# Column sums of phi(k) read from two Strassen operand sums instead of from phi(k)

## The chip, the cores and the metric

The kernel runs on one core of a Trainium2 chip. The metric is device time in microseconds (us); the time of a kernel is the median of its runs, and one further execution is taken by the hardware profiler. The engines are named as the profile names them: PE (matmuls), PEld (the loading of a matmul's weights), DVE (vector engine), ACT (scalar engine), POOL, and SP, whose queue issues nearly all transfers.

## What is computed

Two linear attention blocks, A and B, work on the same x and are mixed by a gate:

```python
g = sigmoid((x * gate_w).sum(-1))                 # x: 2048 x 640, bf16
# for each block, with its own wqkv (640 x 1920) and wo (640 x 640), 32 heads of 20 columns:
q, k, v = split(x @ wqkv)
phi = lambda t: where(t > 0, t + 1, exp(t)) + 1e-6
pq, pk = phi(q), phi(k)
kv  = pk^T v          # per head, 20 x 20
z   = column sums of pk over the 2048 rows, per head
o   = (pq kv) / (pq z + 1e-6)
out = g * (o_A @ wo_A) + (1 - g) * (o_B @ wo_B)
```

## The kernel before

**Stages.** The rows are cut into 16 tiles of 128 (`ST`), the 640 columns into 5 of 128 (`DT`) or two halves of 320 (`HF`). For A, then for B, PE runs through the same stages, in an order written out by hand (`manual_schedule`, lines 704 to 806), and each engine takes its own instructions strictly in that order.

1. `k_chunk` (line 218): k = x wk, ten 128x320 matmuls a tile; `phi` (197) turns it into `pk`, with an exponential on ACT and two operations on DVE.
2. `q_pass` (644): `q_unit` (253) makes 128 columns of q for 1024 rows in ten 128x512 matmuls, and `phi` writes them to `pqT`. A unit called with `lifted` takes its "+1" on ACT (line 202) and has a cheaper second DVE operation (205); otherwise DVE reads PSUM itself (207). A has five units left here, B has ten.
3. The column sums. `z_rows` (370), called in `q_pass` behind the first unit, multiplies a 128x32 tile of ones with each of the 16 row tiles of `pk` and each column half: 32 matmuls, four side by side in four groups of 32 columns of the PE array. DVE then multiplies the sums with the head mask `E4` (line 381) into `zr`. `z_pass` (387), two units later, spreads `zr` with five small matmuls, and DVE copies that to `zsel` (395), the weights of `rec_pass` (468), which makes the denominators ("den"). In A, `gate_pass` (179) stands between the first unit and `z_rows`; it makes the gate's sums ("lg") and their exponentials `ge`.
4. `g_all` (669): G = x^T pk (640 x 640). `g_pass` (281) does the fifth block of columns of x plainly, 32 matmuls. `g_strassen` (323) does the other four by Strassen's scheme in Winograd's form, as seven products of 16 matmuls (`g_prod`, 314), in the order x11 b11, SX2 TK2, x12 b21, SX3 TK3, SX1 TK1, x22 TK4, SX4 b22. The operand sums of x are `SX[1..4]` (`x_sum`, 296, made once, in A) and those of pk are `TK[1..4]` (`k_sum`, 306, made in each block), all by DVE; a `k_sum` has 2560 elements to a partition, an `x_sum` 2048. Between the second and the third product stand eight matmuls of `norm_spread` ("ex", 518).
5. `kv_a` and `m_a` for A (among the k tiles of B), `kvt_mm` (398) and `m_unit` (450) for B: products with wv and wo. `kvt_mm(1, ...)` is the first work of PE behind B's `g_strassen`; its weights are `wvB`.
6. The output, in pairs of row tiles (class `Pair`, 558).

**PSUM** has four slots that `ps` (67) hands out in turn or by number; a slot is free when whoever reads it has done so.

**Buffers of the weights.** `wpool` has one buffer to each tag. A's weights and B's share a tag, so a transfer to B's weights waits until the last reader of the tag's former tile is done. Before, `wvB` is issued on SP behind `kv_a` (line 721) and `woB` at line 725, ahead of B's `q_pass`. `TK` of A lies in `pqT[1]`, still empty then; `TK` of B lies in `xT` (2, 3, 4), and its `TK1` in the buffer of wk.

Of the kernel before, what the change touches and what calls it, by code (L numbers as in the profile page):

```python
# [8 lines left out]
P = 128  # L9
FP32 = mybir.dt.float32  # L10
BF16 = mybir.dt.bfloat16
ACT = mybir.ActivationFunctionType
ALU = mybir.AluOpType
# [9 lines left out]
TW = 4  # L23
# [10 lines left out]
def kernel(  # L34
# [32 lines left out]
    def ps(name, slot=None):  # L67

        return ps_raw(name, slot).bitcast(FP32).rearrange("p (b n) -> p b n", b=2)
# [8 lines left out]
    wo_sb = [None, None]  # L78
    ident = persist.tile([P, P], BF16, name="ident")
    I4 = persist.tile([P, H], BF16, name="I4")  # L80
    E4 = persist.tile([P, D], BF16, name="E4")
    maskE = persist.tile([P, WB[0]], BF16, name="maskE")
    KVA = persist.tile([P, NW, WB[0]], BF16, name="KVA")
    spread = persist.tile([P, P], BF16, name="spread")
# [6 lines left out]
    def flat(t, pattern, inner, at=0):  # L91
        n = hc * inner
        return t[:].rearrange(pattern)[:, at * n:(at + 1) * n].rearrange("p (i n) -> p i n", i=hc)
# [1 line left out]
    S3 = persist.tile([P, 3, hc, ic], BF16, name="S3")  # L95
    SX = {k: S3[:, k - 1] for k in (1, 2, 3)}
    SX[4] = flat(M[1], "p c d -> p (c d)", ic)
    TK = [{k: flat(pqT[1], "p c s -> p (c s)", HF, k - 1) for k in (1, 2, 3, 4)},
          {k: flat(xT, "p c s -> p (c s)", HF, k - 2) for k in (2, 3, 4)}]
    ma_dram = scratch.tile([D, D], BF16, name="ma_dram")  # L100
    lift = persist.tile([P, 1], FP32, name="lift")
    TM = [persist.tile([P, DT, HF], BF16, name="TM0")] + [None] * 3
# [46 lines left out]
    for sign, base in ((1, 0), (-1, Dh - 1)):  # L149
# [1 line left out]
            out=maskE[:], in_=maskE[:], pattern=[[-sign * Dh, WB[0] // Dh], [0, Dh]],  # L151
            compare_op=ALU.is_ge, fill=0.0, base=base, channel_multiplier=sign,
        )
    nc.gpsimd.memset(E4[:], 1.0)
    for r in range(4):
        rows = slice(32 * r, 32 * r + 32)
        for sign, base in ((1, 0), (-1, Dh - 1)):
            nc.gpsimd.affine_select(
                out=E4[rows], in_=E4[rows], pattern=[[sign, D]],
                compare_op=ALU.is_ge, fill=0.0, base=base, channel_multiplier=-sign * Dh,  # L160
            )


    warm = ps("warm", 3)
# [13 lines left out]

    def gate_pass():

        pt = ps("lg")
        for h in range(2):
            by_group(pt[:, 0, h * RB:(h + 1) * RB], gwr, xT, h)
        for b in range(2):
            nc.scalar.activation(out=ge[b][:], in_=pt[:, 0, :], func=ACT.Exp, scale=(-1.0, 1.0)[b])
            nc.vector.tensor_scalar(ge[b][:], ge[b][:], 1.0, 1e30, op0=ALU.add, op1=ALU.min)

    def x_transpose(i, slot, eng, cuts=(0, DT)):
# [60 lines left out]
    def mixed(t, m):  # L249

        return t[:, m::DT]
# [29 lines left out]
    def g_pass(b, c, slot):  # L281

        pt = ps(f"g{'AB'[b]}", slot)
        for i in range(ST):
            for hf in range(2):
                g_mm(c, i, hf, pt)
        for hf in range(2):
            nc.scalar.copy(out=GT[hf][:, c, :], in_=pt[:, hf, 0:HF])

    def g_mm(c, i, hf, pt):  # L290
        nc.tensor.matmul(  # L291
# [4 lines left out]
    def x_sum(k):  # L296

        x11, x21 = [xn[:, 0:hc, n:n + ic] for n in (0, ic)]
        x12, x22 = [xn[:, hc:ST, n:n + ic] for n in (0, ic)]
        a, b, op = {  # L300
            1: (x21, x22, ALU.add), 2: (SX[1], x11, ALU.subtract),
            3: (x11, x21, ALU.subtract), 4: (x12, SX[2], ALU.subtract),
        }[k]
        add_rows(SX[k], a, b, op)

    def k_sum(b, k):

        b11, b12 = [pk[:, 0:hc, n * HF:(n + 1) * HF] for n in range(2)]
        b21, b22 = [pk[:, hc:ST, n * HF:(n + 1) * HF] for n in range(2)]
        t = TK[b]  # L310
        left, right = {1: lambda: (b12, b11), 2: lambda: (b22, t[1]), 3: lambda: (b22, b12), 4: lambda: (b21, t[2])}[k]()
        add_rows(t[k], left, right, ALU.subtract)

    def g_prod(pt, left, right, first):

# [7 lines left out]
    def g_strassen(b, norm):  # L323

        x11, x12 = [xn[:, k:k + hc, 0:ic] for k in (0, hc)]
        x22 = xn[:, hc:ST, ic:2 * ic]
        b11 = pk[:, 0:hc, 0:HF]
        b21, b22 = [pk[:, hc:ST, n * HF:(n + 1) * HF] for n in range(2)]
        lo, hi = GT

        def temp(name):
            return work.tile([P, 2, HF], FP32, tag="osb", name=name, bufs=3)

        def add(dst, pt, sb):
            nc.vector.tensor_tensor(out=dst, in0=pt[:, :, 0:HF], in1=sb[:], op=ALU.add)

        even, odd = ps("gs0", 0), ps("gs1", 1)
        g_prod(even, x11, b11, True)
        p1 = temp("p1")
        nc.scalar.copy(out=p1[:], in_=even[:, :, 0:HF])  # L340
        g_prod(odd, SX[2], TK[b][2], True)
        u2 = temp("u2")
        add(u2[:], odd, p1)
        k_sum(b, 4)
        norm()
        g_prod(even, x12, b21, False)
        nc.scalar.copy(out=lo[:, 0:2, :], in_=even[:, :, 0:HF])
        scale(b, 0)
        scale(b, 1)
        g_prod(odd, SX[3], TK[b][3], False)  # L350
        u3 = temp("u3")
        add(u3[:], odd, p1)
        if b == 0:
            x_sum(4)
        else:
            scale(b, 2)
        even = ps("gs0", 0)
        g_prod(even, SX[1], TK[b][1], True)
        add(hi[:, 2:4, :], even, u3)
        scale(b, 3 if b else 2)  # L360
        g_prod(odd, x22, TK[b][4], False)
        add(lo[:, 2:4, :], odd, p1)
        scale(b, 4 if b else 3)
        g_prod(even, SX[4], b22, False)
        for n in range(2):
            nc.vector.tensor_tensor(out=hi[:, n, :], in0=even[:, n, 0:HF], in1=u2[:, n], op=ALU.add)
        if b == 0:
            scale(b, 4)

    def z_rows(b):  # L370

        pt = ps(f"z{'AB'[b]}")
        for k in range(ST // 4):
            for hf in range(2):
                for j in range(4):
                    nc.tensor.matmul(
                        pt[32 * j:32 * j + 32, hf, 0:HF], lhsT=ones[:], rhs=pk[:, 4 * k + j, hf * HF:(hf + 1) * HF],
                        start=(k == 0), stop=(k == ST // 4 - 1), tile_position=(0, 32 * j),
                    )
        zr = work.tile([P, D], BF16, tag="zr", name="zr")  # L380
        nc.vector.tensor_tensor(
            out=zr[:].rearrange("p (b n) -> p b n", b=2), in0=pt[:, :, 0:HF],
            in1=E4[:].rearrange("p (b n) -> p b n", b=2), op=ALU.mult,
        )
        return zr

    def z_pass(b, zr):

        pt = ps(f"zs{'AB'[b]}")
        for c in range(DT):  # L390
            nc.tensor.matmul(
                pt[:, 0, c * H:(c + 1) * H], lhsT=mixed(zr[:], c), rhs=I4[:], start=True, stop=True,
            )
        zsel = work.tile([P, DT, H], BF16, tag="zsel", name="zsel")
        nc.vector.tensor_copy(out=zsel[:], in_=pt[:, 0, 0:DT * H].rearrange("p (c h) -> p c h", h=H))
        return zsel

    def kvt_mm(b, pt, hf):
# [87 lines left out]
    def add_rows(dst, a, b, op):  # L486
        nc.vector.tensor_tensor(out=dst, in0=a, in1=b, op=op)  # L487
# [153 lines left out]
        wo_sb[b] = wpool.tile([P, NG, D], BF16, tag="wo", name="woB")  # L641
        eng.dma_start(out=wo_sb[b][:KG], in_=wo_dram[b].rearrange("(j p) f -> p j f", p=KG))

    def q_pass(b, units):

        units = list(units)
        q_unit(b, *units.pop(0))
        if b == 0:
            gate_pass()
        zr = z_rows(b)  # L650
        for k in range(2):
            if b == 0:
                x_sum(1 + k)
            q_unit(b, *units.pop(0), b == 0)
        zsel = z_pass(b, zr)
        for k, (m, h) in enumerate(units):
            if b == 0 and k < 2:
                if k:
                    x_sum(3)
                else:  # L660
                    k_sum(0, 2)
            q_unit(b, m, h, b == 0)
            if b == 1 and k == 0:
                k_sum(1, 1)
        if b == 1:
            k_sum(1, 2)
        return zsel

    def g_all(b, zsel):

        g_pass(b, DT - 1, 1)
        k_sum(b, 3)
        rts = rec_pass(b, zsel, 2)
        g_strassen(b, lambda: norm_spread(b, rts, (2, 3)))

# [27 lines left out]

    with tc.manual_schedule():
        k_chunk(0, ST - 2)
        turn[0] = (turn[0] + 1) % 4
        nc.vector.tensor_copy(out=gwr[:], in_=gcol[:, :, None].to_broadcast([P, DT, H]))
        k_chunk(0, ST - 1)
        k_sum(0, 1)
        zsel = q_pass(0, [(m, 1) for m in range(DT)])  # L710
        wq[1] = load_w(1, "q", nc.sync)
        g_all(0, zsel)

        turn[0] = 1
        for i in range(ST):
            k_chunk(1, i)
            if i > 3 and i % 2 == 0:
                m_a(i // 2 - 2)
            if i == 1:
                kv_a()  # L720
                wv[1] = load_w(1, "v", nc.sync)
            if i in (3, 6, 9, 12):
                r0 = (i - 3) // 3 * RB
                p_diff(slice(r0, r0 + RB))
        load_wo(1, nc.sync)
        t1 = wpool.tile([P, hc, HF], BF16, tag="wk", name="T1")
        TK[1][1] = t1[:]
        zsel = q_pass(1, [(m, h) for h in range(2) for m in range(DT)])
        g_all(1, zsel)
        banks.close()  # L730
        outer = ctx.enter_context(late_pool("outer"))
        TM[3] = wpool.tile([P, DT, HF], BF16, tag="wk", name="TM3")
# [104 lines left out]
```

## Time and profile before

| what | value |
|---|---|
| runs | 190.49, 190.9 and 191.43 us, median 190.9 us |
| profiled execution | 191.42 us, its span 189.7 us |
| PE busy | 184.0 us, 97% of the span |
| DVE busy | 152.7 us, 80% |
| ACT busy | 70.5 us, 37% |
| POOL busy | 8.6 us, all in the first two of 40 slices |
| granted PE clock, mean | 0.998 |
| DMA | 15.63 MB; at most 5 GB/s in each slice from 109 to 156 us |

How to read it: the span runs from the first to the last instruction of the profiled execution, 1.7 us less than its time. All times of instructions are counted from the span's start. "Busy" counts an engine from the start of an instruction to its end. Neighbouring instructions of DVE overlap by some 0.08 us, so what one costs in a full queue is the distance from its start to the next one's start, which is a little less than its duration.

### The profile page before, as it was taken

To read this page: it belongs to the slowest core of one execution; us is meant where nothing else is said; L and a number is where in the kernel's file an instruction comes from. 1 tells how busy PE (TensorE), PEld (TensorE's weight loads), DVE (VectorE), ACT (ScalarE), POOL (GpSimd) and SP (SyncE) were. 2 spreads that over 40 slices of the span, in tenths; PEclk is the share of its full clock that TensorE was granted. 3 is DMA by queue.
4 is the path that set the end of the run, shared out by engine and by line. 5 is a ranking of instruction groups with operands and counts; after the bars stand their busy time and mean duration, and the time that the engine had idled before them with its cause. 6 is when DMAs were issued, how large, how long until landed. Compare 5 with 4: busy or idle time off the path is not lost.

```text
span 189.7 us, 3630 instructions
## 1 busy us (share of the span) xinstructions
PE 184.0 (97%) x1490; PEld 124.7 (66%) x1497; DVE 152.7 (80%) x244; ACT 70.5 (37%) x99; POOL 8.6 (5%) x23
## 2 busy tenths in 40 slices
PE   8799999999999999999999999999999999999992
PEld 3566657765567677877775555576777776777771
DVE  1378968899898999789886689799999989787553
ACT  2055446455953500357672445412401611111110
POOL 8900000000000000000000000000000000000000
PEclk9999999999999999999999999999999999999999
DMA  5976438993050000241116600000000003212112
GB/s 181 324 143 87 88 78 273 343 224 101 2 173 0 3 0 0 42 166 32 54 40 218 146 5 0 0 0 3 0 0 3 3 0 108 99 65 77 69 69 73
DMA packets 19802, 15.63 MB, mean 82 GB/s; under 512 B 9546, under 2 KB 19658, under 8 KB 19786
## 3 DMA queue, kind: packets, MB, share of 16 engines
q1 hardware_dynamic: 18922, 14.59, 28.5%
q10 hardware_dynamic: 864, 0.82, 1.3%
q8 instruction: 11, 0.18, 0.4%
q14 instruction: 5, 0.04, 0.1%
HBM read 10.00 MB, written 3.44 MB: 71 GB/s over the span
## 4 chain that ended last, share of the span: by engine, by line
PE 93%; DMA 3%; DVE 1%; ACTq 0%; issue 0%; ACT 0%; DVEq 0%
PE gs L318 16%; PE kB L210 11%; PE qB L259 11%; PE kA L210 11%; PE qA L259 7%; PE ox L548 6%; PE oy L548 5%; PE oz L548 5%; PE qA L270 4%; DMA xn<-in_A_x_dram 3%; PE ow L548 3%; PE gB L291 2%; PE gA L291 2%; DVE osb L553 1%; PE mA L441 1%; PE mid L402 1%
## 5 line engine op out<-in xcount | busy, mean ns | idle before, releaser
L210 PEld LDWEIGHTS <-xT 128*128 128x128 bf16 x320 | 31.0, 98 | 12.3 <-DVE xT L195 0.4
L203 DVE TENSOR_SCALAR e<-e 128x640 bf16<-128x640 bf16 (+1 forms) x52 | 18.8, 361 | 9.6 <-ACT e L200 9.0
L210 PE MATMUL kB<-wkB,xT 128*128 128x320 bf16 x160 | 23.0, 299 | 0.0
L210 PE MATMUL kA<-wkA,xT 128*128 128x320 bf16 x160 | 22.6, 299 | 0.0
L259 PE MATMUL qB<-xT,wqB 128*128 128x512 bf16 x97 | 22.0, 379 | 0.2
L200 ACT ACTIVATE e<-kB 128x640 bf16<-128x640 f32 x16 | 11.3, 704 | 18.8 <-PE kB L210 17.5
L259 PEld LDWEIGHTS <-wqB 128*128 128x128 bf16 x100 | 11.6, 118 | 9.6 <-issue 0.3
L200 ACT ACTIVATE e<-kA 128x640 bf16<-128x640 f32 x16 | 11.1, 704 | 13.6 <-PE kA L210 13.6
L200 ACT ACTIVATE e<-qB 128x1024 bf16<-128x1024 f32 x10 | 10.2, 1024 | 13.2 <-PE qB L259 10.7
L207 DVE SCALAR_TENSOR_TENSOR pk<-kA,e 128x640 bf16<-128x640 f32 x16 | 13.2, 824 | 1.7
L207 DVE SCALAR_TENSOR_TENSOR pk<-kB,e 128x640 bf16<-128x640 f32 x16 | 13.2, 824 | 1.7
L200 ACT ACTIVATE e<-qA 128x1024 bf16<-128x1024 f32 x10 | 10.2, 1024 | 10.6 <-PE qA L259 5.2
L259 PE MATMUL qA<-xT,wqA 128*128 128x512 bf16 x58 | 13.5, 380 | 0.1
L207 DVE SCALAR_TENSOR_TENSOR pqTB<-qB,e 128x1024 bf16<-128x1024 f32 x10 | 12.2, 1224 | 1.0
L318 PEld LDWEIGHTS <-S 128*128 128x128 bf16 x96 | 9.4, 98 | 3.6
L318 PEld LDWEIGHTS <-xn 128*128 128x128 bf16 x96 | 9.1, 98 | 4.0 <-issue 0.4
L592 ACT COPY u<-ox 128x320 f32<-128x320 f32 x8 | 3.4, 426 | 21.9 <-PE ox L548 21.9
L259 PEld LDWEIGHTS <-wqA 128*128 128x128 bf16 x60 | 6.9, 118 | 5.6 <-issue 0.3
L548 PEld LDWEIGHTS <-xT 128*128 128x128 bf16 x85 | 8.0, 98 | 3.1 <-DVE xT L487 0.2
L548 PEld LDWEIGHTS <-pqTA 128*128 128x128 bf16 x85 | 7.9, 98 | 2.9 <-issue 0.2
L548 PEld LDWEIGHTS <-pqTB 128*128 128x128 bf16 x80 | 7.8, 98 | 3.0
L576 ACT COPY p1s<-ox 128x320 f32<-128x320 f32 x8 | 3.4, 426 | 16.6 <-PE ox L548 16.6
(121 smaller groups left out, 287.7 us busy)
## 6 DMA issues: line engine op xcount, KB each, us to landing
out_dram<-osb SPq DMA_DIRECT2D x14, 160.0 KB, 1.8
xn<-in_A_x_dram SPq DMA_DIRECT2D x3, 640.0 KB, 7.2
wqA<-in_A_wqkv_dram SPq DMA_DIRECT2D x1, 800.0 KB, 6.5
wvA<-in_A_wqkv_dram SPq DMA_DIRECT2D x1, 800.0 KB, 11.0
wkB<-in_B_wqkv_dram SPq DMA_DIRECT2D x1, 800.0 KB, 5.8
wqB<-in_B_wqkv_dram SPq DMA_DIRECT2D x1, 800.0 KB, 4.5
wvB<-in_B_wqkv_dram SPq DMA_DIRECT2D x1, 800.0 KB, 4.6
MA<-ma_dram SPq DMA_DIRECT2D x1, 800.0 KB, 4.4
```

The lines of the kernel that those rows point to most:

```text
L200: nc.scalar.activation(out=e[:], in_=src, func=ACT.Exp)
L203: nc.vector.tensor_scalar(e[:], e[:], 1.0, EPS, op0=ALU.min, op1=ALU.add)
L207: nc.vector.scalar_tensor_tensor(out=dst, in0=src, scalar=1.0 + EPS, in1=e[:], op0=ALU.add, op1=ALU.max)
L210: nc.tensor.matmul(pt[:, hf, 0:HF], lhsT=xT[:, c, i * P:(i + 1) * P], rhs=wk[b][:, c, hf * HF:(hf + 1) * HF], start=(c == 0), stop=(c == D ...
L259: nc.tensor.matmul(pt[:, u, :], lhsT=mixed(wq[b][:, c, :], m), rhs=xT[:, c, n * HB:(n + 1) * HB], start=(c == 0), stop=(c == DT - 1),)
L270: nc.tensor.matmul(pt[:, u, :], lhsT=mixed(wq[b][:, c, :], m + u), rhs=xT[:, c, n * HB:(n + 1) * HB], start=(c == 0), stop=(c == DT - 1),)
L291: nc.tensor.matmul(pt[:, hf, 0:HF], lhsT=xn[:, i, c * P:(c + 1) * P], rhs=pk[:, i, hf * HF:(hf + 1) * HF], start=(i == 0), stop=(i == ST - 1),
L318: nc.tensor.matmul(pt[:, n, 0:HF], lhsT=left[:, i, n * P:(n + 1) * P], rhs=right[:, i, :], start=(first and i == 0), stop=(i == hc - 1), s ...
L402: nc.tensor.matmul(pt[:KG, hf, j * KG:(j + 1) * KG], lhsT=wv[b][:, c, (4 * hf + j) * KG:(4 * hf + j + 1) * KG], rhs=GT[hf][:, c, j * KG:(j ...
L548: nc.tensor.matmul(dst, lhsT=left[:, c, r0:r0 + P], rhs=right[:, c, :], start=(first and c == 0), stop=(c == DT - 1), skip_group_check=not ...
L576: nc.scalar.copy(out=self.p1s[:], in_=self.at("x"))
L592: nc.scalar.copy(out=self.u2[:], in_=self.at("x"))
```

## The change

The column sums are no longer taken from `pk`. Two operand sums of Strassen's scheme hold them already, once the signs are turned: with b11, b12, b21, b22 the quarters of pk (first digit: half of the rows; second: half of the columns), TK3 is now b22 + b12 and TK4 is now b11 + b21 - b12 - b22. The column sums of TK3 are those of the right half of pk, and those of TK3 + TK4 are those of the left half. Both have eight row tiles, not 16, so `z_rows` has 16 matmuls. For the products to stay what they were, SX1, SX2 and SX3 change their signs too.

- `z_rows` and `z_pass` move from `q_pass` into `g_pass`: the first behind 12 of its 32 matmuls, the second behind 28. In A, `x_sum(1)`, `gate_pass` and `x_sum(2)` follow `z_rows` there, and `x_sum(3)` moves behind the second product of `g_strassen`.
- The sums come out of PSUM by two ACT copies of 128x320 and one DVE addition of 128x320. The head mask is applied behind `z_pass`, by a DVE multiplication with `headE` (128x32) in the place of the copy to `zsel`; `E4` and its eight selections on POOL go.
- All four `k_sum`s of a block are now made inside `q_pass`, before `g_pass`. In B, three of ten units are lifted.
- B's TK1 lies in the buffer of wv, TK2 and TK3 in that of wo, TK4 in that of wk. So `woB` is now issued behind the fourth product of B's `g_strassen` (SX3 TK3) and `wvB` behind the fifth (SX1 TK1).

The diff, without the parts that only rename or delete a tile:

```diff
@@ -95,8 +95,7 @@
-    TK = [{k: flat(pqT[1], "p c s -> p (c s)", HF, k - 1) for k in (1, 2, 3, 4)},
-          {k: flat(xT, "p c s -> p (c s)", HF, k - 2) for k in (2, 3, 4)}]
+    TK = [{k: flat(pqT[1], "p c s -> p (c s)", HF, k - 1) for k in (1, 2, 3, 4)}, {}]
@@ -151,14 +150,12 @@
             out=maskE[:], in_=maskE[:], pattern=[[-sign * Dh, WB[0] // Dh], [0, Dh]],
             compare_op=ALU.is_ge, fill=0.0, base=base, channel_multiplier=sign,
         )
-    nc.gpsimd.memset(E4[:], 1.0)
-    for r in range(4):
-        rows = slice(32 * r, 32 * r + 32)
-        for sign, base in ((1, 0), (-1, Dh - 1)):
-            nc.gpsimd.affine_select(
-                out=E4[rows], in_=E4[rows], pattern=[[sign, D]],
-                compare_op=ALU.is_ge, fill=0.0, base=base, channel_multiplier=-sign * Dh,
-            )
+    nc.gpsimd.memset(headE[:], 1.0)
+    for sign, base in ((1, 0), (-1, TW - 1)):
+        nc.gpsimd.affine_select(
+            out=headE[:], in_=headE[:], pattern=[[-sign * TW, H]],
+            compare_op=ALU.is_ge, fill=0.0, base=base, channel_multiplier=sign,
+        )
 
 
     warm = ps("warm", 3)
@@ -178,11 +175,11 @@
 
     def gate_pass():
 
-        pt = ps("lg")
+        pt = ps("lg", 2)
         for h in range(2):
-            by_group(pt[:, 0, h * RB:(h + 1) * RB], gwr, xT, h)
+            by_group(pt[:, 1, h * RB:(h + 1) * RB], gwr, xT, h)
         for b in range(2):
-            nc.scalar.activation(out=ge[b][:], in_=pt[:, 0, :], func=ACT.Exp, scale=(-1.0, 1.0)[b])
+            nc.scalar.activation(out=ge[b][:], in_=pt[:, 1, :], func=ACT.Exp, scale=(-1.0, 1.0)[b])
             nc.vector.tensor_scalar(ge[b][:], ge[b][:], 1.0, 1e30, op0=ALU.add, op1=ALU.min)
 
     def x_transpose(i, slot, eng, cuts=(0, DT)):
@@ -282,10 +279,19 @@
 
         pt = ps(f"g{'AB'[b]}", slot)
         for i in range(ST):
+            if i == 6:
+                zt, zr = z_rows(b, 0)
+                if b == 0:
+                    x_sum(1)
+                    gate_pass()
+                    x_sum(2)
+            if i == 14:
+                zsel = z_pass(zt, zr)
             for hf in range(2):
                 g_mm(c, i, hf, pt)
         for hf in range(2):
             nc.scalar.copy(out=GT[hf][:, c, :], in_=pt[:, hf, 0:HF])
+        return zsel
 
     def g_mm(c, i, hf, pt):
         nc.tensor.matmul(
@@ -298,8 +304,8 @@
         x11, x21 = [xn[:, 0:hc, n:n + ic] for n in (0, ic)]
         x12, x22 = [xn[:, hc:ST, n:n + ic] for n in (0, ic)]
         a, b, op = {
-            1: (x21, x22, ALU.add), 2: (SX[1], x11, ALU.subtract),
-            3: (x11, x21, ALU.subtract), 4: (x12, SX[2], ALU.subtract),
+            1: (x21, x22, ALU.subtract), 2: (x11, SX[1], ALU.subtract),
+            3: (x21, x11, ALU.subtract), 4: (x12, SX[2], ALU.subtract),
         }[k]
         add_rows(SX[k], a, b, op)
 
@@ -309,7 +315,7 @@
         b21, b22 = [pk[:, hc:ST, n * HF:(n + 1) * HF] for n in range(2)]
         t = TK[b]
         left, right = {1: lambda: (b12, b11), 2: lambda: (b22, t[1]), 3: lambda: (b22, b12), 4: lambda: (b21, t[2])}[k]()
-        add_rows(t[k], left, right, ALU.subtract)
+        add_rows(t[k], left, right, ALU.add if k in (2, 3) else ALU.subtract)
 
     def g_prod(pt, left, right, first):
 
@@ -341,13 +347,16 @@
         g_prod(odd, SX[2], TK[b][2], True)
         u2 = temp("u2")
         add(u2[:], odd, p1)
-        k_sum(b, 4)
+        if b == 0:
+            x_sum(3)
         norm()
         g_prod(even, x12, b21, False)
         nc.scalar.copy(out=lo[:, 0:2, :], in_=even[:, :, 0:HF])
         scale(b, 0)
         scale(b, 1)
         g_prod(odd, SX[3], TK[b][3], False)
+        if b == 1:
+            load_wo(1, nc.sync)
         u3 = temp("u3")
         add(u3[:], odd, p1)
         if b == 0:
@@ -356,6 +365,8 @@
             scale(b, 2)
         even = ps("gs0", 0)
         g_prod(even, SX[1], TK[b][1], True)
+        if b == 1:
+            wv[1] = load_w(1, "v", nc.sync)
         add(hi[:, 2:4, :], even, u3)
         scale(b, 3 if b else 2)
         g_prod(odd, x22, TK[b][4], False)
@@ -367,32 +378,35 @@
         if b == 0:
             scale(b, 4)
 
-    def z_rows(b):
-
-        pt = ps(f"z{'AB'[b]}")
-        for k in range(ST // 4):
-            for hf in range(2):
+    def z_rows(b, slot):
+
+        pt = ps(f"z{'AB'[b]}", slot)
+        for k in range(hc // 4):
+            for hf, t in enumerate((TK[b][4], TK[b][3])):
                 for j in range(4):
                     nc.tensor.matmul(
-                        pt[32 * j:32 * j + 32, hf, 0:HF], lhsT=ones[:], rhs=pk[:, 4 * k + j, hf * HF:(hf + 1) * HF],
-                        start=(k == 0), stop=(k == ST // 4 - 1), tile_position=(0, 32 * j),
+                        pt[32 * j:32 * j + 32, hf, 0:HF], lhsT=ones[:], rhs=t[:, 4 * k + j, :],
+                        start=(k == 0), stop=(k == hc // 4 - 1), tile_position=(0, 32 * j),
                     )
         zr = work.tile([P, D], BF16, tag="zr", name="zr")
-        nc.vector.tensor_tensor(
-            out=zr[:].rearrange("p (b n) -> p b n", b=2), in0=pt[:, :, 0:HF],
-            in1=E4[:].rearrange("p (b n) -> p b n", b=2), op=ALU.mult,
-        )
-        return zr
-
-    def z_pass(b, zr):
-
-        pt = ps(f"zs{'AB'[b]}")
+        upper = work.tile([P, HF], FP32, tag="ex", name="zu")
+        nc.scalar.copy(out=upper[:], in_=pt[:, 1, 0:HF])
+        nc.scalar.copy(out=zr[:, HF:D], in_=pt[:, 1, 0:HF])
+        nc.vector.tensor_tensor(out=zr[:, 0:HF], in0=pt[:, 0, 0:HF], in1=upper[:], op=ALU.add)
+        return pt, zr
+
+    def z_pass(pt, zr):
+
+        dst = pt[:, 0, HF:HF + DT * H]
         for c in range(DT):
             nc.tensor.matmul(
-                pt[:, 0, c * H:(c + 1) * H], lhsT=mixed(zr[:], c), rhs=I4[:], start=True, stop=True,
+                dst[:, c * H:(c + 1) * H], lhsT=mixed(zr[:], c), rhs=I4[:], start=True, stop=True,
             )
         zsel = work.tile([P, DT, H], BF16, tag="zsel", name="zsel")
-        nc.vector.tensor_copy(out=zsel[:], in_=pt[:, 0, 0:DT * H].rearrange("p (c h) -> p c h", h=H))
+        nc.vector.tensor_tensor(
+            out=zsel[:], in0=dst.rearrange("p (c h) -> p c h", h=H),
+            in1=headE[:, None, :].to_broadcast([P, DT, H]), op=ALU.mult,
+        )
         return zsel
 
     def kvt_mm(b, pt, hf):
@@ -641,35 +655,16 @@
         wo_sb[b] = wpool.tile([P, NG, D], BF16, tag="wo", name="woB")
         eng.dma_start(out=wo_sb[b][:KG], in_=wo_dram[b].rearrange("(j p) f -> p j f", p=KG))
 
-    def q_pass(b, units):
-
-        units = list(units)
-        q_unit(b, *units.pop(0))
-        if b == 0:
-            gate_pass()
-        zr = z_rows(b)
-        for k in range(2):
-            if b == 0:
-                x_sum(1 + k)
-            q_unit(b, *units.pop(0), b == 0)
-        zsel = z_pass(b, zr)
+    def q_pass(b, units, sums, lifted):
+
         for k, (m, h) in enumerate(units):
-            if b == 0 and k < 2:
-                if k:
-                    x_sum(3)
-                else:
-                    k_sum(0, 2)
-            q_unit(b, m, h, b == 0)
-            if b == 1 and k == 0:
-                k_sum(1, 1)
-        if b == 1:
-            k_sum(1, 2)
-        return zsel
-
-    def g_all(b, zsel):
-
-        g_pass(b, DT - 1, 1)
-        k_sum(b, 3)
+            q_unit(b, m, h, k in lifted)
+            if k in sums:
+                k_sum(b, sums[k])
+
+    def g_all(b):
+
+        zsel = g_pass(b, DT - 1, 1)
         rts = rec_pass(b, zsel, 2)
         g_strassen(b, lambda: norm_spread(b, rts, (2, 3)))
 
@@ -703,13 +698,12 @@
 
     with tc.manual_schedule():
         k_chunk(0, ST - 2)
-        turn[0] = (turn[0] + 1) % 4
         nc.vector.tensor_copy(out=gwr[:], in_=gcol[:, :, None].to_broadcast([P, DT, H]))
         k_chunk(0, ST - 1)
         k_sum(0, 1)
-        zsel = q_pass(0, [(m, 1) for m in range(DT)])
+        q_pass(0, [(m, 1) for m in range(DT)], {0: 2, 1: 3, 2: 4}, (1, 2, 3, 4))
         wq[1] = load_w(1, "q", nc.sync)
-        g_all(0, zsel)
+        g_all(0)
 
         turn[0] = 1
         for i in range(ST):
@@ -718,15 +712,16 @@
                 m_a(i // 2 - 2)
             if i == 1:
                 kv_a()
-                wv[1] = load_w(1, "v", nc.sync)
             if i in (3, 6, 9, 12):
                 r0 = (i - 3) // 3 * RB
                 p_diff(slice(r0, r0 + RB))
-        load_wo(1, nc.sync)
-        t1 = wpool.tile([P, hc, HF], BF16, tag="wk", name="T1")
-        TK[1][1] = t1[:]
-        zsel = q_pass(1, [(m, h) for h in range(2) for m in range(DT)])
-        g_all(1, zsel)
+        turn[0] = 2
+        TK[1][1], TK[1][4] = [wpool.tile([P, hc, HF], BF16, tag=t, name=n)[:] for t, n in (("wv", "T1"), ("wk", "T4"))]
+        t = wpool.tile([P, 2, hc, HF], BF16, tag="wo", name="T23")
+        TK[1][2], TK[1][3] = t[:, 0], t[:, 1]
+        k_sum(1, 1)
+        q_pass(1, [(m, h) for h in range(2) for m in range(DT)], {0: 2, 2: 3, 4: 4}, (3, 5, 7))
+        g_all(1)
         banks.close()
         outer = ctx.enter_context(late_pool("outer"))
         TM[3] = wpool.tile([P, DT, HF], BF16, tag="wk", name="TM3")
```

More of the change, by code (lines that the diff above doesn't have):

```diff
@@ L80 @@
     I4 = persist.tile([P, H], BF16, name="I4")
-    E4 = persist.tile([P, D], BF16, name="E4")
+    headE = persist.tile([P, H], BF16, name="headE")
     maskE = persist.tile([P, WB[0]], BF16, name="maskE")
```

## The prediction

> **What bounds the kernel now.** I read the page's busy shares first, then the chain of waits in order of time, then DVE's timeline where the change moves work, then the transfers.
>
> ```profile
> PE 184.0 (97%) x1490; PEld 124.7 (66%) x1497; DVE 152.7 (80%) x244; ACT 70.5 (37%) x99; POOL 8.6 (5%) x23
> ```
>
> PE is busy 97% of 189.7 us, and from 7.1 to 183.4 us the chain is PE's matmuls back to back. So a matmul taken away is worth its own time, as long as nothing that PE waits for gets late. The chain where the change works (start, duration, line, count):
>
> ```profile
> 41.49 1.21 PE lg L174 x39
> 42.70 1.09 PE zA L376 x32
> ...
> 52.74 4.35 PE gA L291 x32
> 57.09 1.21 PE denA L174 x40
> ...
> 101.15 1.20 PE zB L376 x32
> ...
> 132.51 10.97 PE gs L318 x80
> 143.48 0.77 PE mid L402 x20
> ```
>
> The reader is to see that "mid", the first work with wvB, starts the moment the last Strassen product ends. There is no slack there.
>
> **Part 1: the matmuls.** 32 matmuls take 1.09 us, 0.034 each, since four run side by side; zB's 1.20 holds a change of stage. Sixteen less are 0.55 us in each block. Changes between matmuls of a quarter array and whole ones are as many as before (seven in A, six in B), so they cancel. The five small matmuls stay. Gain: 0.55 in A, 0.55 in B, if nothing waits.
>
> **Part 2: block A, DVE's queue.** What DVE does, with the real cost as the distance between starts:
>
> ```profile
> 41.31 1.48 DVE L487 TENSOR_TENSOR pqTB<-pk 128x2560 bf16<-128x2560 bf16 x1
> 42.71 0.42 DVE L203 TENSOR_SCALAR e<-e 128x1024 bf16<-128x1024 bf16 x1
> 43.23 1.23 DVE L207 SCALAR_TENSOR_TENSOR pqTA<-qA,e 128x1024 bf16<-128x1024 f32 x1
> 44.37 0.42 DVE L186 TENSOR_SCALAR geA<-geA 128x512 f32<-128x512 f32 x1
> ...
> 50.44 0.69 DVE L205 TENSOR_TENSOR pqTA<-pqTA,e 128x1024 bf16<-128x1024 bf16 x1
> 51.05 0.32 DVE L395 CAST zsel<-zsA 128x160 bf16<-128x160 f32 x1
> ```
>
> A k_sum costs 1.40, a plain unit's phi 1.66 (0.52 and 1.14), a lifted one's 1.13 (0.52 and 0.61), an x_sum 1.14 (48.78 to 49.91), each `ge` 0.33. In the new order DVE has from 41.31: four k_sums (5.60), one plain phi (1.66), four lifted (4.54). That ends at 53.1 without a pause. TK4, behind the second lifted unit, is ready at 50.9. PE: five units of 2.17 from 39.33 end at 50.2, twelve gA matmuls (0.136 each) at 51.8, so `z_rows` waits for nothing. Then z 0.55, lg 1.21, sixteen gA, the small five 0.17, four gA: PE would begin "den" at 56.5.
>
> "Den" needs `zsel`, and DVE is late with it. Behind 53.1 stand, in the order of the program: the addition to zr (0.42; the row of a 128x320 addition on line 553 is 0.50 long), x_sum(1) 1.14, both ge 0.67, x_sum(2) 1.14, then zsel, 0.32 long. That ends at 56.8. ACT's copies and exponentials (0.43 and 0.60 each) are done by 54.7, and hold nothing up. With 0.1 for the semaphore and the weights, "den" begins at 56.9 to 57.0, against 57.09 before. So of A's 0.55 only **0.15** is left; the new wait has x_sum(2) in front of it. Bounds: 0.55 (no wait) and 0 (it comes at 57.1). Behind "den" the order is as before, with an x_sum (1.14) in the place of a k_sum (1.40) on DVE, so nothing gets later.
>
> **Part 3: block B up to its end.** B has ten units of 2.17 on PE, and DVE has four k_sums, seven plain phis, three lifted: 5.6 + 11.6 + 3.4 = 20.6 us against 21.7 of PE. By adding up as in A, TK4 is ready some 8 us before `z_rows`, the last phi 2 us before zsel, and "den" does not wait. Unit 2 takes the slot of k tile 15, whose phi ends at 101.02; PE wants it at 101.16, so at most a tenth is lost. ACT's three more "+1" (1.11 each) lie in its pauses of 1.13 between units. Gain **0.50**, bounds 0.40 and 0.60. POOL's work (8.6 us at the start) is first needed at 45 us: its loss is worth nothing. The k_sums that leave g_strassen are off the path too.
>
> **Part 4: the transfers of woB and wvB.** This is the dear part. SP's timeline and the view of the transfers (KB each, us from issue to landing), and two windows of 1 us:
>
> ```profile
> 100.44 0.35 SPq L448 DMA_DIRECT2D MA<-ma_dram  x1
> 100.88 0.38 SPq L642 DMA_DIRECT2D woB<-in_B_wo_dram  x1
> ```
>
> ```profile
> wvB<-in_B_wqkv_dram SPq DMA_DIRECT2D x1, 800.0 KB, 4.6
> MA<-ma_dram SPq DMA_DIRECT2D x1, 800.0 KB, 4.4
> woB<-in_B_wo_dram SPq DMA_DIRECT2D x1, 800.0 KB, 7.2
> ```
>
> ```profile
> 81.00:82.00 1.00, 1.00 (x10) 0.72 (x8) 0.90 (x2) 0.70 (x1) 0.00 (x0) 1.00 1.07 397
> 106.00:107.00 1.00, 1.00 (x10) 0.66 (x9) 0.90 (x2) 0.16 (x1) 0.00 (x0) 1.00 0.99 196
> ```
>
> Before, wvB was issued at 78.4 and landed 60 us ahead of its use. Now SP waits for PE twice: woB goes out when SX3 TK3 is done, wvB when SX1 TK1 is done. Behind them on SP stand only the stores of the output. In the times of before, with 0.137 us a matmul: 132.51 + 32 x 0.137 = 136.9 and 139.1. PE wants wvB at 143.5, that is 4.4 us after its issue. Alone it takes 4.6. And it is not alone: woB, issued 2.2 us ahead, is slow to move (last number of the last two rows: wvB 397 GB/s, woB 196, both with the engines full). Three prices:
> - Nothing of woB in the way: 139.1 + 4.6 = 143.7, a wait of 0.25.
> - The pair in the trace that is like it: MA and woB, 1.6 MB, landed 7.64 us after the first issue (100.44 to 108.08). From 136.9 that is 144.6, a wait of 1.1. Adding up gives more: 1.0 to the first bytes, some 0.5 of slow start, 4.1 for 0.82 MB of woB at 200 GB/s, 2.1 for wvB at 390, 0.5 to the landing, 8.2 in all: a wait of 1.6.
> - wvB as long as woB took behind MA, 7.2: 146.3, a wait of 2.85.
>
> I take **1.35**, between the two sums of the middle case, and 0.05 for PE to load its weights again. woB itself is needed only 3 us later and is there. Nothing behind "mid" gets earlier for it, as all of it is PE's chain again.
>
> **The sum**: -0.15 - 0.50 + 1.40 = +0.75 us. The profiled execution took 191.42 (span 189.7 and 1.7 around it), so it would take 192.2. It is the upper end of the runs shown; against their median of 190.9 the forecast is **191.6 us**. About 0.5% (0.95 us) is what a measurement of this kernel can tell from no change.
>
> **Rivals.**
> - *wvB is much later* (slower). Its packets queue behind all of woB's and crawl as woB's do. Past a wait of 1.65 us the change is measurably slower; at 2.85 the sum is +2.25, 193.2 us. For it: woB's 7.2 us. Against: wvB's own 397 GB/s, and its start is hidden behind woB.
> - *wvB is nearly on time* (faster). If woB moves as fast as wvB, 2.2 us of woB are done when wvB starts; a wait of 0.3 leaves 191.42 - 0.65 + 0.3, or 190.5 by the median. If zsel too comes in time, -0.9, 190.0. Against: the 196 GB/s row.
> - *PE's clock falls at the wait*. The trace shows a slow PE only at its start: the seven warm-up matmuls (128x512) take 3.14 us, where such matmuls later take 0.217 each, 1.5 in all. If the wait for wvB brought that back for as long, it would cost 1.6 us more: +2.35, 193.2. Against: the granted clock is 0.998 in the mean, and behind PE's pause of 0.97 us at 7.15 ten kA matmuls take 1.37, full pace. The Trainium skill (TensorE: Matmul & The Clock Gate, What's actually happening) halves the clock only after an idle window of about 3.4 us; by that rule a wait of this size costs no clock, and the trace agrees as far as 0.97 us goes.
>
> That the sums are not halved is no rival: the program's order shows 16 matmuls to a block.
>
> **How the numbers follow.** The forecast (a wait of 0.6 to 1.65) 0.48; wvB much later 0.33; the clock 0.04; wvB nearly on time 0.15. Of the last, half comes out more than 0.5% faster, with the noise of runs that differ by 0.9 us. So faster 0.07, same 0.56, slower 0.37. The bounds of the costs: best -0.55 - 0.60 + 0.25 = -0.9, worst 0 - 0.40 + 2.90 = +2.5; the range is 190.0 to 193.4 us.
>
> **What would show it.** Right: PE waits in front of "mid" for the transfer of wvB, over 0.6 us; it waits some 0.4 us in front of A's "den" for DVE's zsel, behind x_sum(2); no wait in front of B's "den"; zA and zB with 16 matmuls in some 0.55 us. Wrong: wvB landing in time, or a wait inside B's units. The forecast falls if the two transfers share the engines otherwise than MA and woB did.

## The result and the profile after

The changed kernel takes 192.09 us (median of 12 runs), the kernel before 190.78 (12 runs): a ratio of 1.0072, with a 95% interval of 1.0046 to 1.0098. By the ratio that is 1.37 us more, with the interval 0.9 to 1.9; the medians lie 1.31 apart. (Here and below, the microseconds beside a ratio are what it makes of the kernel before's median.) The profiled execution took 192.37 us, its span 190.5.

The busy line of the page:

```profile
PE 183.7 (96%) x1460; PEld 124.2 (65%) x1465; DVE 150.3 (79%) x244; ACT 75.0 (39%) x106; POOL 2.8 (1%) x17
```

PE has 30 matmuls fewer in its records and is less busy, and still the span is longer: the time is in PE's pauses. Its timeline has two with a releaser in the changed stretch (start, duration, then in brackets the pause before and what ended it):

```profile
56.45 1.28 PE L171 MATMUL denA<-pqTA,zsel 128*32 128x256 bf16 x40 [0.46 <-DVE zsel L406]
...
144.10 0.96 PE L416 MATMUL mid<-GT,wvB 128*80 128x80 bf16 x20 [1.66 <-DMA wvB<-in_B_wqkv_dram]
```

These are the two waits that the prediction named, in front of A's "den" and of "mid". The chain of waits in order of time shows how each comes about:

```profile
49.61 1.63 PE gA L297 x12
51.24 0.69 PE zA L387 x16
51.95 0.43 ACT zu L393
52.38 0.33 ACT zr L394
...
55.03 0.47 DVE S L501
...
56.08 0.33 DVE zsel L406
56.45 1.28 PE denA L171 x40
...
131.46 6.64 PE gs L324 x48
138.12 5.93 DMA wvB<-in_B_wqkv_dram
144.10 0.96 PE mid L416 x20
```

In A the chain leaves PE at the column sums, goes through two copies on ACT and a row of DVE work that ends with x_sum(2) and zsel, and comes back to PE at "den". (The first `k_sum` of each block stands just ahead of `q_pass`, not inside it as the section on the change has it; the prediction's queue has it in the right place.) In B it leaves PE in the middle of the Strassen products, where wvB is issued, and stays with the transfer until "mid".

To see what each stage gained or lost, I take distances on the chain, since the time up to A's q matmuls differs from run to run (38.6 to 40.0 us in the nine profiles of this case):

| from, to (us) | before | after | difference |
|---|---|---|---|
| span's start to A's q matmuls | 39.33 | 38.82 | -0.51 |
| to A's first Strassen product | 18.96 | 18.91 | -0.05 |
| to B's q matmuls | 40.71 | 40.71 | 0.00 |
| to B's first Strassen product | 28.66 | 28.17 | -0.49 |
| to "mid" | 15.82 | 17.49 | +1.67 |
| to the end of the span | 46.22 | 46.40 | +0.18 |

Without the first row the sum is +1.31 us, which agrees with the runs (+1.37). Most of the last row lies in the first matmuls of "mid": the first 20 take 0.96 us behind the wait and 0.77 before, the second 20 take 0.82 and 0.85, and from the start of "mid" to the first product with woB it is 3.14 us, not 2.98, so 0.16 us more. That distance comes out the same in every profile, 3.13 to 3.15 with a wait and 2.97 to 2.98 without. The whole last row does not: it is 45.9 to 46.4 us in the nine profiles, whether there was a wait or not.

### The profile page after: what moved, and what is told of

It reads as the page before. It is cut to its first block, busy times and chain, and to the rows that moved or that the text cites. A ratio compares the mean times of both kernels' runs of the same rounds, so it can differ in the third digit from the quotient of the medians.

```text
span 190.5 us, 3574 instructions
## 1 busy us (share of the span) xinstructions
PE 183.7 (96%) x1460; PEld 124.2 (65%) x1465; DVE 150.3 (79%) x244; ACT 75.0 (39%) x106; POOL 2.8 (1%) x17
## 4 chain that ended last, share of the span: by engine, by line
PE 91%; DMA 3%; DVE 3%; issue 1%; ACT 1%; DVEq 0%; ACTq 0%
PE gs L324 14%; PE kA L207 12%; PE kB L207 11%; PE qB L256 11%; PE qA L256 7%; PE ox L562 6%; PE oy L562 5%; PE oz L562 5%; PE qA L267 4%; DMA wvB<-in_B_wqkv_dram 3%; PE ow L562 2%; PE gB L297 2%; PE warm L164 2%; DVE osb L567 1%; PE mid L416 1%; DVE S L501 1%
## 5 line engine op out<-in xcount | busy, mean ns | idle before, releaser
L207 PE MATMUL kA<-wkA,xT 128*128 128x320 bf16 x160 | 23.2, 304 | 0.0
L324 PE MATMUL gs<-pk,xn 128*128 128x320 bf16 x64 | 9.4, 300 | 0.0
```

What stands on the lines that cost most here:

```text
L207: nc.tensor.matmul(pt[:, hf, 0:HF], lhsT=xT[:, c, i * P:(i + 1) * P], rhs=wk[b][:, c, hf * HF:(hf + 1) * HF], start=(c == 0), stop=(c == D ...
L324: nc.tensor.matmul(pt[:, n, 0:HF], lhsT=left[:, i, n * P:(n + 1) * P], rhs=right[:, i, :], start=(first and i == 0), stop=(i == hc - 1), s ...
```

## The experiments

All ratios are against the kernel before, from runs on the same chip.

**e1: wvB issued early.** B's second operand sum lies in wv's buffer, the first and third in wo's. So wvB goes out behind the second product and woB behind the fifth. The edit is shortened here ("..."); the two calls of the loads, which move with it, are left out.

```diff
-        TK[1][1], TK[1][4] = [... (("wv", "T1"), ("wk", "T4"))]
-        t = wpool.tile([P, 2, hc, HF], BF16, tag="wo", name="T23")
-        TK[1][2], TK[1][3] = t[:, 0], t[:, 1]
+        TK[1][2], TK[1][4] = [... (("wv", "T2"), ("wk", "T4"))]
+        t = wpool.tile([P, 2, hc, HF], BF16, tag="wo", name="T13")
+        TK[1][1], TK[1][3] = t[:, 0], t[:, 1]
```

> Theory: what is lost is the wait for wvB at the end of B's Strassen products, 1.66 us in the profile of the changed kernel, and some 0.2 us of slower first matmuls behind it. With TK2 in wv's buffer, wvB is issued behind the second product, some 8 us earlier, lands long before it is wanted, and woB, issued behind the fifth, lands in about 6 us, just before its first matmul: 1.37 - 1.85 = -0.5 us against the kernel before. Rival: the loss lies in the moved sums and in the new order of DVE and ACT; then at least +0.9 us stays.

Measured: 0.9978 (0.9955 to 1.0001), -0.4 us. From B's first product to "mid" it takes 15.82 us again, as before the change. The chain:

```profile
137.99 4.48 PE gs L324 x33
142.47 0.76 PE mid L416 x20
```

"Mid" follows the last product without a gap, and its 20 matmuls are back to 0.76. The theory holds: without the wait and the slow start behind it the change loses nothing against the kernel before. What it could gain is not all there yet, though, since PE still waits 0.46 us for zsel in A.

**e2: x_sum(2) behind zsel, in A.**

```diff
                     gate_pass()
-                    x_sum(2)
             if i == 14:
                 zsel = z_pass(zt, zr)
+                if b == 0:
+                    x_sum(2)
```

> Only x_sum(2) moved behind zsel in A. Theory: the wait of 0.46 us in front of A's denominators is DVE finishing x_sum(2) before zsel; it goes, so +0.95 us against the kernel before (0.4 less than the changed kernel's +1.37), and denA starts 0.4 us sooner behind the last q matmul. Rival: something else holds zsel (the ACT copies, the five small matmuls), and the time stays at +1.37.

Measured: 1.0034 (1.0015 to 1.0053), +0.65 us. DVE's timeline of this run:

```profile
54.75 0.42 DVE L183 TENSOR_SCALAR geB<-geB 128x512 f32<-128x512 f32 x1
55.69 0.33 DVE L407 TENSOR_TENSOR zsel<-zA,headE 128x160 bf16<-128x160 f32 x1 [0.52 <-PE zA L403]
55.93 1.22 DVE L502 TENSOR_TENSOR S<-xn,S 128x2048 bf16<-128x2048 bf16 x1
```

DVE now waits for PE's five small matmuls, not PE for DVE, and "den" has no pause. From A's q matmuls to its first product it takes 18.39 us, 0.52 less than in the changed kernel: the wait of 0.46, and 0.07 because "den" takes 1.21 us and not 1.28 as behind the wait. So x_sum(2) did stand in the way. The time came out below the expected +0.95, though that lies in the interval (+0.3 to +1.0); the profile has 0.3 of it in B, where wvB landed 5.6 us after its issue and PE waited 1.34 us, which this edit does not explain.

**e3: both edits.**

> Both edits. Theory: the two waits are separate and add up: -0.9 us against the kernel before (189.9 where before is 190.8), near the whole worth of 32 fewer matmuls (1.1). Rival: removing one uncovers another, -0.5 at best.

Measured: 0.9944 (0.9921 to 0.9966), 190.03 against 191.09 us, -1.07 us. The two waits add up: e1 takes off 1.8 us of the changed kernel's time, e2 0.7, both 2.4. From A's q matmuls to its first product this version takes 18.38 us and in B 28.16, so 0.58 and 0.50 less than before, near the 0.55 that sixteen matmuls are worth. Without the waits the change is faster than the kernel before, and this version beats both kernels.

**e4: the kernel before, with the two transfers late.** The edit without the two calls that now issue the loads; the comments are mine.

```diff
-                wv[1] = load_w(1, "v", nc.sync)          # behind kv_a; now behind SX1 TK1
...
-        load_wo(1, nc.sync)                              # ahead of B's q; now behind SX3 TK3
-        t1 = wpool.tile([P, hc, HF], BF16, tag="wk", name="T1")
+        t23 = wpool.tile([P, 2, hc, HF], BF16, tag="wo", name="T23")
+        TK[1][2], TK[1][3] = t23[:, 0], t23[:, 1]
+        t1 = wpool.tile([P, hc, HF], BF16, tag="wv", name="T1")
```

> The kernel before with its 32 matmuls for the sums, but TK1 in wv's buffer and TK2, TK3 in wo's, so that woB and wvB are issued as late as in the changed kernel, and nothing else of the change. Theory: +1.85 us against before, with PE waiting 1.6 to 1.7 us for wvB. Rival (the other edits cost the time): +0.5 us at most.

Measured: 1.0094 (1.0068 to 1.0121), +1.8 us. PE's timeline:

```profile
145.50 0.96 PE L406 MATMUL mid<-GT,wvB 128*80 128x80 bf16 x20 [1.56 <-DMA wvB<-in_B_wqkv_dram]
```

The transfers by themselves, with nothing else of the change, bring the wait and the price.

**e5: the kernel before, with wvB alone late.** As e4, but woB stays where it was and only TK1 lies in wv's buffer.

> The kernel before, with TK1 in wv's buffer: wvB alone is issued late, behind the fifth product, and woB stays early. Theory: most of the 1.6 us is woB's transfer, slow and in front of wvB's; alone wvB lands 4.6 to 4.9 us after its issue, 4.4 us before PE wants it, so PE waits 0.3 to 0.5 us and the time is +0.5 to +0.7 us against before. Rival: the late issue alone does it; then wvB lands 5.6 to 5.9 us after it, as behind woB, and the time is +1.7 us or more.

Measured: 1.0022 (1.0000 to 1.0045), +0.4 us. The view of the transfers and PE's timeline:

```profile
wvB<-in_B_wqkv_dram SPq DMA_DIRECT2D x1, 800.0 KB, 4.6
```

```profile
143.86 0.96 PE L404 MATMUL mid<-GT,wvB 128*80 128x80 bf16 x20 [0.33 <-DMA wvB<-in_B_wqkv_dram]
```

Issued at the same point, wvB lands 4.6 us after its issue when it is alone, and 5.8 behind woB (e4). So of e4's wait of 1.56 us, 0.33 is the late issue and the rest is woB ahead of it, and the runs agree: 1.4 us lie between e4 and e5. The rival, the late issue alone, falls. The 4.6 us are no fixed figure, though: alone, wvB took them in the kernel before, e5 and e6, but 5.2 in e1 and 5.7 in e3, where it was early enough for that to cost nothing. So the split is that of one execution; what the 12 runs say of the late issue alone is 0.0 to 0.9 us, far below the 1.7 of the rival.

**e6: e3 with the sums' 16 matmuls made twice**, and **e7: the changed kernel with them made twice.**

```diff
-        for k in range(hc // 4):
+        for k in [*range(hc // 4)] * 2:
             for hf, t in enumerate((TK[b][4], TK[b][3])):
```

> The version with both waits removed, its 16 matmuls of the column sums made twice in each block (the second time from the start, so the sums are the same). Theory: with no wait left, 16 matmuls cost 0.55 us in each block, +1.1 us against the version with both edits, so about 0 against the kernel before. Rival: A's matmuls lie beside DVE's work, and only B's 0.55 is seen: -0.5 us against before.

> The changed kernel with its 16 matmuls of the column sums made twice. Theory: in A most of the added 0.55 us lies in the 0.46 us in which PE waits for zsel, since DVE ends x_sum(2) at the same time, so A pays 0.1 to 0.2 and its wait shrinks to nothing; in B the 0.55 us delays the issue of woB and wvB as much as PE, so it is paid in full: +0.7 us against the changed kernel, +2.0 to +2.1 against before. Rival: both are paid, +1.1 against the changed kernel, +2.5 against before.

Measured: e6 1.0020 (0.9996 to 1.0044), +0.4 us; e7 1.0127 (1.0102 to 1.0151), +2.4 us. The interval of e6 is wide for what is asked, so the stages decide: from A's q matmuls to its first product e6 takes 18.92 us against 18.38 in e3, and from B's q matmuls to its first product 28.71 against 28.16. Sixteen matmuls are 0.54 or 0.55 us in each block, as was expected of e6. In e7 it is 19.45 against 18.91 in A and 28.71 against 28.17 in B: also paid in full, and A's wait is what it was:

```profile
56.79 1.28 PE L171 MATMUL denA<-pqTA,zsel 128*32 128x256 bf16 x40 [0.46 <-DVE zsel L406]
```

Here my theory fell and the rival was right. I had taken DVE's queue to be what makes zsel late, so that longer column sums would hide beside it. But the wait stays at 0.46 us when PE's sums take 0.54 longer, so the row of DVE work behind them starts when they are done. The chain of the changed kernel says so: from zA to ACT's copies to DVE without a stretch of DVE's earlier work in it. DVE's last phi of A begins at 51.98 and would let the next operation in at 52.59, by the usual distance of 0.61; the addition to zr begins at 52.73, behind ACT's second copy. The rows of DVE and ACT in the changed kernel:

```profile
51.98 0.69 DVE L202 TENSOR_TENSOR pqTA<-pqTA,e 128x1024 bf16<-128x1024 bf16 x1
52.73 0.49 DVE L395 TENSOR_TENSOR zr<-zA,zu 128x320 bf16<-128x320 f32 x1
```

```profile
52.27 0.43 ACT L394 CAST zr<-zA 128x320 bf16<-128x320 f32 x1
```

## Why the prediction was right, and what was mis-sized

The forecast of 191.6 us (+0.75 us) was on the right side, its range holds 192.09, and the mechanism is the one named. What was off is the size of terms, above all of one: of the 0.56 us between +0.75 and the table's +1.31, 0.45 lie in the transfers and 0.10 in block A.

- **The matmuls.** 0.55 in each block: measured 0.54 and 0.55 (e6, e7). The chain has 0.69 us for zA and 0.66 for zB, since each also holds a change of stage.
- **Block A**, -0.15: measured -0.05. "Den" was forecast at 56.9 to 57.0, so 17.57 to 17.67 us behind the start of A's q matmuls (39.33), and begins 17.63 us behind it, with a wait of 0.46 behind x_sum(2), as said (e2). What the sum had left out is that "den" itself is slower behind the wait, 1.28 us for 1.21. Wrong too was what starts the row: the prediction let DVE's queue end at 53.1, and wrote that ACT's copies "hold nothing up". Counted from A's q matmuls DVE's queue did end as forecast, 13.8 us on; but the copies hold the row up (e7), by 0.14 us only, which is why the sum was still near. That was luck.
- **Block B**, -0.50: measured -0.49, with no wait in front of its "den".
- **The transfers**, +1.40: measured +1.67 for the wait and 0.16 for slow matmuls behind it, 1.83 in all; the runs have 1.8 (e4, and e1 against the changed kernel). This is the mis-sized term. The wait differs from one execution to the next: with woB ahead of wvB it is 1.34, 1.53, 1.56 and 1.66 us in four profiles (e2, e7, e4, the changed kernel), so the 1.35 taken was at the low end and not out of reach. The prediction had two sums for the middle case, and took a value between them: 7.64 us from the first issue to the second landing, from the pair MA and woB, and 8.2 added up from the rates. SP's timeline and the view of the transfers of the changed kernel:

```profile
135.95 0.33 SPq L656 DMA_DIRECT2D woB<-in_B_wo_dram  x1
138.12 0.39 SPq L641 DMA_DIRECT2D wvB<-in_B_wqkv_dram  x1
```

```profile
woB<-in_B_wo_dram SPq DMA_DIRECT2D x1, 800.0 KB, 6.1
wvB<-in_B_wqkv_dram SPq DMA_DIRECT2D x1, 800.0 KB, 5.9
```

From 135.95 to 138.12 + 5.9 = 144.0 is 8.1 us (7.8 to 8.0 in e2, e4 and e7): the sum from the rates was nearer than the pair. There woB came second and 0.44 us behind MA, here it comes first and 2.17 us ahead; which of the two makes the difference no run shows. The sum was near in part by luck. Its terms were a slow start of 0.5 us and 200 GB/s for all of woB. In the changed kernel woB's first piece moves 1.0 us after its issue, as assumed, but some 1.1 us more pass before the engines are fully busy. And woB does not move at 200 GB/s throughout. The first window of 1 us with full engines has 334 GB/s, and that is woB alone, since wvB is issued at 138.12 and its first piece came 1.05 to 1.06 us after its issue wherever it was alone; only the next windows have 221 and 228. The other part of the error is the 0.05 for PE's start behind the wait, which was 0.16. In both blocks, then, PE's slow start behind a wait was put too low.

The rivals: *wvB much later* was priced at a wait of 2.85 and begins at 1.65. The measured 1.66 is just past that edge, and so just outside the stretch of 0.6 to 1.65 that the forecast gave itself; and the change is slower by more than 0.5%, where the prediction gave that 0.37 and no change 0.56. But wvB did not crawl: once the engines are its own it has 361 GB/s. *wvB nearly on time* fell because woB is slow, as the row of 196 GB/s had it, but only in its second half:

```profile
138.00:139.00 1.00, 1.00 (x9) 0.71 (x8) 0.87 (x2) 0.00 (x0) 0.00 (x0) 1.00 1.05 334
139.00:140.00 1.00, 1.00 (x10) 0.72 (x8) 1.00 (x1) 0.00 (x0) 0.00 (x0) 1.00 1.11 221
140.00:141.00 1.00, 1.00 (x9) 0.73 (x8) 0.79 (x2) 0.00 (x0) 0.00 (x0) 1.00 1.10 228
...
142.00:143.00 1.00, 0.44 (x4) 0.10 (x1) 0.78 (x3) 0.00 (x0) 0.00 (x0) 1.00 1.06 361
...
144.00:145.00 1.00, 0.90 (x21) 0.90 (x22) 0.00 (x0) 0.00 (x0) 0.00 (x0) 1.00 0.00 0
```

(The last three numbers are the granted PE clock, the busy share of the DMA engines and GB/s.) *PE's clock falls* did not happen: the granted clock is 1.00 in the windows behind the wait, and the five ox matmuls after "mid" take 0.68 us, as before. A pause of 1.66 us agrees with the rule of the Trainium skill (TensorE: Matmul & The Clock Gate, What's actually happening) that only a longer idle window lowers it.

## What to carry to other kernels

A buffer lent to a temporary is paid for by the transfer that wants it back: look at when the last reader ends, and at what else is issued in the same stretch. Here the same three buffers, with two of the temporaries exchanged, turned +1.37 us into -0.4. Where work is moved behind a short dependent step on another engine, put what nobody waits for yet (x_sum(2)) behind that step and not in front of it. And a price taken from one pair of transfers need not hold for another order or spacing: the pair gave 7.64 us, this one took 7.8 to 8.1 in four profiles. PE's start behind a wait is a term of its own, 0.16 us here.

## What the runs showed of the hardware that was not expected

- Two transfers of 800 KB each, wvB to 128 partitions and woB to 80, with pieces of the same 1280 bytes: alone, wvB lands in 4.6 to 5.7 us (five profiles) and woB in 5.7 (e1, e3, e6). They start alike and end differently. In windows of half a microsecond with full engines, woB's first has 338 to 387 GB/s (the changed kernel, e1, e3, e6) and its last ones 197 to 236; wvB, alone, has 353 to 404 from first to last (e1, e3, e5, e6). So a rate read from one window is not that of the transfer. Why woB slows down, and whether the number of partitions is the cause, was not tried. In e3, where they come one behind the other, with wvB in the first of these windows of 1 us and woB in the other two:

```profile
133.00:134.00 1.00, 1.00 (x9) 0.73 (x8) 1.00 (x2) 0.69 (x1) 0.00 (x0) 1.00 1.01 370
...
140.00:141.00 1.00, 1.00 (x10) 0.71 (x8) 1.00 (x2) 0.00 (x0) 0.00 (x0) 1.00 1.11 287
141.00:142.00 1.00, 1.00 (x17) 0.83 (x15) 0.79 (x2) 0.00 (x0) 0.00 (x0) 1.00 1.10 221
```

- The first 20 small matmuls of "mid" take 0.96 us behind a wait for their weights, 0.76 to 0.77 without one (five profiles and four), after a wait of 1.66 us as after one of 0.33 (e5), with the granted clock at 1.00. So it is a price of the wait and not of its length. What it consists of stays open.
